# Linear attention and a Swish MLP on one core: batch 1's v loaded ahead of w_out's third quarter, its x transposed by DMA, batches 2 and 3 loaded behind it, batch 0's two norms back to back

## The chip, the cores and the metric

One Trainium2 chip, one of its cores. The engines go by short names: PE multiplies matrices, DVE (vectors) and ACT (exp, silu and the like) work on its results and inputs, POOL issues the loads and SP the stores and the DMA transposes. PSUM is the buffer that PE's products go to, which the kernel hands out in pairs of banks; SBUF is the memory that the loads fill. The granted clock is the share of its full rate that PE's clock was given. The metric is device time in microseconds (us) of one execution, median of several; lower is better. All experiments are timed beside the kernel before on the same chip; sets of runs were on different chips, so ratios are compared rather than times.

## The reference

```python
# q, k, v: (8, 8, 576, 64) f32; w_in: (512, 2048), w_out: (2048, 512), beta: (2048,)
def phi(x): return np.where(x > 0, x, np.exp(x) - 1.0) + 1.0
kv  = einsum('bhsd,bhse->bhde', phi(k), v)
num = einsum('bhsd,bhde->bhse', phi(q), kv)
den = einsum('bhsd,bhd->bhs', phi(q), sum(phi(k), axis=2)) + 1e-6
x = (num / den).transpose(0, 2, 1, 3).reshape(4608, 512)
h = x @ w_in
out = (h * sigmoid(beta * h)) @ w_out
```

## The kernel before

Names used below: **h(b)** is the first product of batch b (x times w_in, 16 slices of 128 columns of w_in, then silu on ACT), **y(b)** the second (g times w_out); **kv(b)** the 40 small products of phi(k) and v; **numerators** the products of phi(q) and kv, followed on DVE by the division (num_norm), which gives the normed rows; these must be transposed to become **x(b)**, the input of h(b). While the MLP of batch b runs on PE, the attention of batch b + 1 is slipped in between by a plan: at which step which function is emitted. The plan is read as the schedule: every engine is taken to do its work in the order of emission.

```python
def load_rows(dst, src, b, eng=nc.gpsimd):        # POOL's queue; f32 in memory, bf16 in SBUF
    eng.dma_start(out=dst[:, :, 0:NJ, :]..., in_=src[b, :, 0:MAIN, :]...)      # 512 KB
    eng.dma_start(out=dst[0:TAIL, :, NJ, :], in_=src[b, :, MAIN:S, :]...)      # 64 KB

def by_dma(b):
    return b >= DMA_T                              # DMA_T = 2: x(0), x(1) go through PE
def num_norm(b, t):
    ...                                            # den, reciprocal, xs = num * 1/den
    if by_dma(b) or t == NJ:
        nc.sync.dma_start_transpose(out=x_dst(b, t), in_=xs...)                # SP's queue
def x_trans(b, t, wide=False, dve=False):          # 4 PE transposes and one copy from PSUM
    ...
def h_last(b, x, between):                         # last 4 slices of h; they use the PSUM
    hps = []                                       # pairs that kv and numerators use too
    for i in range(2):
        hp = att_banks()
        for ii in range(2):
            h_mm(b, x, hp[:, ii], 12 + 2 * i + ii, 0, 4)
            hps.append(hp[:, ii])
    for f in between:
        f()                                        # exp of the next batch on ACT
    for i in range(4):
        silu(b, 12 + i, hps[i])                    # frees the PSUM pairs
def hold(a):
    nc.gpsimd.tensor_copy(held, a)                 # POOL, and so its loads, wait until a is there
# ... cut: start, h(0)
load_w_out(2)
load_v(1)
load_w_out(3)
# ... cut
load_next(2)                                       # k, q, v of batch 2
h_last(0, xT[0], [])
# ... cut: exp, relu, phi of batch 1
y_phase_wide(0, {
    4: [F(load_next, 3)],
    10: [F(q_trans, 1, 0, 1, 2, 3), F(kv_mm, 1), F(kv_evac, 1), F(w_out_scale, 3, 2)],
    11: [F(num_mm, 1, 0), F(num_norm, 1, 0)],
    12: [F(num_mm, 1, 1), F(num_norm, 1, 1), F(x_trans, 1, 0, wide=True)],
    # ... cut
})
h_phase(1, ...)
h_last(1, xT[1], [F(exp_, 2, 0), F(exp_, 2, 1)])   # exp of q(2), of k(2)
exp_(3, 1); exp_(3, 0); silu_table()
y_phase_wide(1, {
    1: [F(phi, 2, 0), F(q_trans_dma, 2), F(phi, 2, 1)],
    6: [F(kv_mm, 2), F(kv_evac, 2)],
    8: [F(num_mm, 2, 0), F(num_norm, 2, 0)],
    # ... cut
})
```

Of the kernel before, what the change touches and what calls it, by code (L numbers as in the profile page):

```python
# [16 lines left out]
def kernel(  # L17
# [12 lines left out]
    B, H, S, D = q.shape  # L30
# [3 lines left out]
    KC = DM // P  # L34
    FC = DFF // P
    NJ = 4
# [1 line left out]
    TAIL = S - MAIN  # L38
    NT = NJ + 1
    EA = D + 2  # L40
    DMA_T = 2
    TINY = 2.0 ** -30

    ctx.enter_context(tc.manual_schedule())
# [15 lines left out]
    HH = H // 2  # L60
# [5 lines left out]
    xT = [consts.tile([P, NJ, KC, P], BF16, name=f"xT{i}") for i in range(3)]  # L66
# [4 lines left out]
    def load_rows(dst, src, b, eng=nc.gpsimd):  # L71
        eng.dma_start(  # L72
            out=dst[:, :, 0:NJ, :].rearrange("p h j d -> p h (j d)"),
            in_=src[b, :, 0:MAIN, :].rearrange("h (p j) d -> p h (j d)", j=NJ),
        )
        eng.dma_start(
            out=dst[0:TAIL, :, NJ, :],
            in_=src[b, :, MAIN:S, :].rearrange("h s d -> s h d"),
        )

    def load_q(b):
        load_rows(xqk[b % NX][:, 0], q, b)

    def load_k(b):
        load_rows(xqk[b % NX][:, 1], k, b)

    def load_v(b):
        load_rows(vraw[b % 2], v, b)
# [19 lines left out]
    def load_w_out(i):  # L108
        for ii in range(2):
            c0 = 4 * i + 2 * ii  # L110
            nc.gpsimd.dma_start(out=w_out_f[i][ii], in_=w_out_v[:, c0 : c0 + 2, :])
# [92 lines left out]
        nc.vector.tensor_add(beta_c, beta_s, beta_m)  # L204
        nc.vector.reciprocal(rbeta, beta_c)

    def w_out_scale(i, on_dve=4):
        for c in range(4):
            ff = 4 * i + c
            dst, src, by = w_out_sb[i][:, c, :], w_out_f[i][c // 2][:, c % 2, :], rbeta[:, ff : ff + 1]  # L210
            if c < on_dve:
                nc.vector.tensor_scalar(dst, src, by, None, ALU.mult)
            else:
                nc.scalar.activation(dst, src, ACTF.Copy, scale=by)  # L214
# [1 line left out]

    st = {}

    def by_dma(b):
        return b >= DMA_T  # L220

    def begin(b):
        st[b, "p"] = work.tile([P, 2, NT, DM], BF16, tag="qk_p", name="qk_p")
# [17 lines left out]
    def phi(b, a, h0=0, h1=H):  # L241
        nc.vector.tensor_tensor(  # L242
            st[b, "p"][:, a].rearrange("p j (h d) -> p h j d", h=H)[:, h0:h1],
            st[b, "r", a][:, h0:h1], st[b, "e", a][:, h0:h1], ALU.min,
        )
# [9 lines left out]
    def work9(tag, **kw):  # L255
        return nine(work.tile([P, H, NT, D], BF16, tag=tag, name=tag, **kw), "jhd")

    def in9(a, j0, j1):
        if a == 1 and j0 >= KF:
            return k_last[:, :, j0 - KF : j1 - KF]  # L260
        return x9[a][:, :, j0:j1]

    def exp9(a, j0, j1):
        if j0 == 0:
            st["e9", a] = work9("e", bufs=3)
        nc.scalar.activation(
            st["e9", a][:, j0:j1].rearrange("p j h d -> p h j d"), in9(a, j0, j1),
            ACTF.Exp,
        )

    def relu9(a, j0, j1):
        if j0 == 0:
            st["r9", a] = work9("r")
        nc.vector.tensor_scalar(
            st["r9", a][:, j0:j1].rearrange("p j h d -> p h j d"), in9(a, j0, j1),
            0.0, 1.0, ALU.max, ALU.add,
        )
# [68 lines left out]
    def v_copy(b, h0=0, h1=H, dve=True):  # L346
        copy(
            vaug[b % 2][:, :, h0:h1, 0:D].rearrange("p j h d -> p h j d"),
            vraw[b % 2][:, h0:h1], dve,
        )  # L350
# [32 lines left out]
    def copy(dst, src, dve):  # L383
        if dve:
            nc.vector.tensor_copy(dst, src)  # L385
        else:
            nc.scalar.activation(dst, src, ACTF.Copy)  # L387
# [40 lines left out]
    def num_norm(b, t):  # L428
        n = P
        den = work.tile([P, 2, 4], F32, tag="den", name="den")  # L430
        rden = work.tile([P, 2, 4], F32, tag="rden", name="rden")
        xs = work.tile([P, 2, 4, D], BF16, tag="xs", name="xs", bufs=4)
        st[b, "xs", t] = xs
        nv = st[b, "n", t][:n, :, 0 : 4 * (D + 1)].rearrange("p a (h e) -> p a h e", h=4)
        nc.vector.tensor_scalar(den[:n], nv[:, :, :, D], 1e-6, None, ALU.add)  # L435
        nc.vector.reciprocal(rden[:n], den[:n])  # L436
        nc.vector.tensor_mul(  # L437
            xs[:n], nv[:, :, :, 0:D], rden[:n, :, :, None].to_broadcast([n, 2, 4, D])
        )
        if by_dma(b) or t == NJ:  # L440
            nc.sync.dma_start_transpose(
                out=x_dst(b, t), in_=xs.rearrange("p a h d -> p (a h d)")[:n]
            )
# [6 lines left out]
    def x_trans(b, t, wide=False, dve=False):  # L450
        n = P
        xv = st[b, "xs", t].rearrange("p a h d -> p (a h d)")
        tp = tr_bank(wide)[:, 0 : KC * P].rearrange("p (c n) -> p c n", c=KC)
        for p in range(KC):
            nc.tensor.matmul(  # L455
                tp[:, p, :n], xv[:n, p * P : (p + 1) * P], identity[:n, :n],
                is_transpose=True, start=True, stop=True, skip_group_check=True,
            )
        copy(x_dst(b, t), tp[:, :, :n], dve)
# [122 lines left out]
            y_out(b, t, yp[t], on_act=True)  # L582
            run(plan, 12 + t)

    def load_next(b):
        if b < B:
            load_k(b)
            load_q(b)
            load_v(b)

    held = consts.tile([1, 1], BF16)

    def hold(a):

        nc.gpsimd.tensor_copy(held, a)  # L595
# [14 lines left out]
    def warm(n):  # L610
        for _ in range(n):
            nc.tensor.matmul(  # L612
                st["warm"], g_sb[0][:, FC - 1, 0:P], g_sb[0][:, FC - 1, :],
                start=True, stop=True, skip_group_check=True,
            )

    def silu_table():
        nc.scalar.activation(small[:, 1:2], small[:, 0:1], ACTF.Silu)

    def F(f, *a, **k):  # L620
        return lambda: f(*a, **k)
# [31 lines left out]
    num_mm(0, 0)  # L653
    num_mm(0, 1)
    num_norm(0, 0)
    exp9(0, QF, N9)
    relu9(0, QF, N9)
    silu_table()
    warm(4)
    x_trans(0, 0, dve=True)  # L660
    num_norm(0, 1)
    phi9(0, QF, 6)
    phi9(0, 6, N9)
    qb2 = att_banks(BF16)


    load_w_out(2)
    load_v(1)
    load_w_out(3)

    def tidy():
# [3 lines left out]
    def q_rest():  # L675
        for t in range(2, NT):
            q_trans9(t, qb2, (t - 2) * 256)
        for t in range(2, NT):
# [5 lines left out]
        + [(ff, 0, 2) for ff in range(4, 8)] + [(ff, 2, 4) for ff in range(8)]  # L684
        + [(ff, 0, 4) for ff in range(8, 12)],
        {
            1: [F(x_trans, 0, 1)],
            3: [F(q_rest)],
            5: [F(num_mm, 0, 2), F(num_norm, 0, 2)],
            7: [F(num_mm, 0, 3), F(num_norm, 0, 3)],  # L690
# [5 lines left out]


    clear_tail(2)
    load_next(2)
    h_last(0, xT[0], [])  # L700
    begin(1)
    exp_(1, 1)
    exp_(1, 0)
    silu_table()
    relu(1, 1)
    relu(1, 0)
    w_out_scale(2)
    phi(1, 1)
    phi(1, 0)
    v_copy(1, 0, HH)  # L710
    v_copy(1, HH, H, dve=False)
    y_phase_wide(0, {
        4: [F(load_next, 3)],
        10: [
            F(q_trans, 1, 0, 1, 2, 3), F(kv_mm, 1), F(kv_evac, 1), F(w_out_scale, 3, 2),
        ],
        11: [F(num_mm, 1, 0), F(num_norm, 1, 0)],
        12: [F(num_mm, 1, 1), F(num_norm, 1, 1), F(x_trans, 1, 0, wide=True)],
        13: [F(num_mm, 1, 2), F(num_norm, 1, 2), F(x_trans, 1, 1, wide=True)],
        14: [F(num_mm, 1, 3), F(num_norm, 1, 3), F(q_trans, 1, 4)],  # L720
    })

    ALL = [(ff, 0, 4) for ff in range(FC)]
    h_phase(
        1, xT[1],
        [(ff, 0, 2) for ff in range(4)] + [(ff, 2, 4) for ff in range(4)] + ALL[4:12],
        {
            0: [F(x_trans, 1, 2), F(num_mm, 1, 4), F(num_norm, 1, 4)],
            1: [F(x_trans, 1, 3)],
            8: [F(begin, 2), F(relu, 2, 0)],  # L730
            10: [F(relu, 2, 1)],
            12: [F(v_copy, 2), F(load_v, 4)],
        },
    )
    begin(3)
# [3 lines left out]
    silu_table()  # L739
    y_phase_wide(1, {  # L740
        1: [F(phi, 2, 0), F(q_trans_dma, 2), F(phi, 2, 1)],
        6: [F(kv_mm, 2), F(kv_evac, 2)],
        8: [F(num_mm, 2, 0), F(num_norm, 2, 0)],
        9: [F(num_mm, 2, 1), F(num_norm, 2, 1)],
        10: [F(num_mm, 2, 2), F(num_norm, 2, 2)],
# [3 lines left out]
    for b in range(2, B + 1):  # L749
        n = b + 1  # L750
        groups = ALL
        plan = {}
        if b == 2:
            groups = (
                [(ff, 0, 2) for ff in range(8)] + [(ff, 2, 4) for ff in range(8)] + ALL[8:]
            )
        o = len(groups) - FC
        if n < B:
            plan[3 + o] = [F(relu, n, 0), F(phi, n, 0), F(q_trans_dma, n)]
            plan[5 + o] = [F(relu, n, 1), F(phi, n, 1)]  # L760
            plan[7 + o] = [F(v_copy, n), F(held_v, b + 3, n)]
            plan[12 + o] = [F(kv_mm, n)]
            plan[13 + o] = [F(kv_evac, n)]
        h_phase(b, xT[b % 3] if b < B else xT_tail, groups, plan)
        plan = {}
        if n + 1 < B:
            begin(n + 1)
            exp_(n + 1, 1)
            exp_(n + 1, 0)
        if n < B:  # L770
            for t in range(NT if n % 2 else NJ):
                plan[1 + 2 * t] = [F(num_mm, n, t)]
                plan[2 + 2 * t] = [F(num_norm, n, t)]
            plan[12] = [F(held_kq, b + 3, n)]
        y_phase(b, plan)
# [30 lines left out]
```

## Time and profile before

| | before |
|---|---|
| time, median of 3 runs (lowest to highest) | 292.67 us (292.13 to 292.94) |
| span of the profiled execution | 290.1 us |
| PE busy | 281.8 us (97%) |
| first h matmul / y(0) / h(1) / y(1) / h(2) starts on PE | 17.09 / 33.36 / 51.56 / 66.44 / 82.04 us |
| granted PE clock, mean | 0.994 |

The last row is from PE's timeline and serves as a ruler: what a stage costs is the distance between two of its entries.

### The profile page before, as it was taken

The numbers are of one execution on the slowest core, as the hardware profiler recorded it, in microseconds if no ns is written. First come the engines' busy times: TensorE is split into PE (matmuls) and PEld (weight loads), VectorE is DVE, ScalarE is ACT, GpSimd is POOL, SyncE is SP. The second block draws the span as 40 slices with busy tenths as digits, with TensorE's granted clock in tenths as the row PEclk, the third lists the DMA queues.
The fourth block names the chain that finished last, engine by engine and source line by source line (L and its number), as shares of the span: only waits on it lengthen the run. The fifth ranks groups of instructions, "written<-read, shape, count | busy, mean of one in ns | idle before, by whom it ended". The sixth has DMA issues, their size and how long they took to land.

```text
span 290.1 us, 4739 instructions
## 1 busy us (share of the span) xinstructions
PE 281.8 (97%) x1895; PEld 144.1 (50%) x1895; DVE 116.7 (40%) x235; ACT 174.0 (60%) x232; POOL 54.3 (19%) x79
## 2 busy tenths in 40 slices
PE   8889999999999999999999999999999999999994
PEld 3567445644576444454444444554455444444443
DVE  3784487504670365326532654163517300110021
ACT  2788798889998843875277617771750086018500
POOL 8924564400051205020402040000000000000000
PEclk9799999999999999999999999999999999999999
DMA  8999999999379956977894879433503500120033
GB/s 143 196 206 345 254 281 194 257 167 158 62 208 180 136 140 106 196 103 162 121 211 53 161 92 197 77 103 107 97 2 90 111 36 0 72 76 0 0 74 73
DMA packets 75766, 38.07 MB, mean 131 GB/s; under 512 B 43344, under 2 KB 70240, under 8 KB 75744
## 3 DMA queue, kind: packets, MB, share of 16 engines
q0 software_dynamic: 38912, 20.19, 49.0%
q1 hardware_dynamic: 36640, 17.44, 25.7%
q8 instruction: 15, 0.25, 0.4%
q10 hardware_dynamic: 192, 0.14, 0.2%
q14 instruction: 7, 0.06, 0.1%
HBM read 36.71 MB, written 9.44 MB: 159 GB/s over the span
## 4 chain that ended last, share of the span: by engine, by line
PE 92%; DMA 3%; POOL 3%; ACT 1%; issue 0%; DVE 0%; POOLq 0%
PE mm L527 42%; PE mm L475 41%; PE att L421 3%; DMA w_in<-in_moe_w_in_dram 3%; PE att L475 2%; PE att L362 2%; POOL xqk L135 1%; PE mm L559 1%; POOL vraw L135 1%; ACT q_pT L387 1%; PE mm L455 0%; PE att L395 0%; PE att L455 0%; DVE xT L385 0%; DVE y_sb L385 0%
## 5 line engine op out<-in xcount | busy, mean ns | idle before, releaser
L467 ACT ACTIVATE g<-mm,beta_c 128x512 bf16<-128x512 f32 (+2 forms) x160 | 97.8, 623 | 87.1 <-PE mm L475 87.0
L527 PE MATMUL mm<-w_out,g 128*128 128x512 bf16 x560 | 128.0, 379 | 0.0
L475 PE MATMUL mm<-xT,w_in 128*128 128x512 bf16 (+2 forms) x576 | 107.6, 344 | 1.3 <-DMA w_in<-in_moe_w_in_dram 1.2
L475 PEld LDWEIGHTS <-w_in 128*128 128x128 bf16 x672 | 63.8, 98 | 60.8 <-DMA w_in<-in_moe_w_in_dram 1.3
L527 PEld LDWEIGHTS <-g 128*128 128x128 bf16 x560 | 53.1, 98 | 59.0 <-issue 0.3
L537 DVE COPY y_sb<-mm 128x512 f32<-128x512 f32 x27 | 18.7, 692 | 72.9 <-PE mm L527 69.4
L229 ACT ACTIVATE e<-xqk 128x2560 bf16<-128x2560 bf16 x14 | 31.9, 2328 | 0.1
L242 DVE TENSOR_TENSOR qk_p<-r,e 128x2560 bf16<-128x2560 bf16 x14 | 20.8, 1491 | 12.8 <-ACT e L229 12.1
L437 DVE TENSOR_TENSOR xs<-att,rden 128x512 bf16<-128x512 f32 x36 | 24.9, 691 | 1.2
L372 DVE CAST kv_bd<-att 64x260 bf16<-64x260 f32 x14 | 6.0, 427 | 36.6 <-PE att L362 36.5
L435 DVE TENSOR_SCALAR den<-att 128x8 f32<-128x8 f32 x36 | 5.9, 163 | 26.8 <-PE att L421 26.8
L421 PEld LDWEIGHTS <-q_pT 128*128 128x128 bf16 (+1 forms) x160 | 11.1, 102 | 9.5 <-issue 1.3
L421 PE MATMUL att<-kv_bd,q_pT 128*128 128x130 bf16 (+1 forms) x160 | 14.8, 226 | 0.4 <-ACT q_pT L387 0.3
L475 PE MATMUL mm<-xT_tail,w_in 128*128 128x512 bf16 x64 | 14.0, 379 | 0.0
L595 POOL COPY held<-xT 1x1 bf16<-1x1 bf16 x4 | 2.0, 509 | 63.6 <-DMA xT<-xs 63.6
L237 DVE TENSOR_SCALAR r<-xqk 128x2560 bf16<-128x2560 bf16 x14 | 11.9, 853 | 4.0 <-DMA xqk<-in_q_dram 2.5
L612 PE MATMUL mm<-g 128*128 128x512 bf16 x30 | 9.3, 464 | 1.2 <-DVE g L145 1.2
L229 ACT ACT_TABLE_LOAD x7 | 9.0, 1283 | 0.1
L72 POOL DMA_DIRECT2D vraw<-in_v_dram x7 | 6.4, 909 | 10.1 <-DVE vaug L385 4.2
L72 POOL DMA_DIRECT2D xqk<-in_q_dram x7 | 7.1, 1021 | 3.9 <-ACT w_out L214 2.1
L436 DVE RECIPROCAL rden<-den 128x8 f32<-128x8 f32 x36 | 7.3, 203 | 1.2
L72 POOL DMA_DIRECT2D xqk<-in_k_dram x7 | 6.5, 935 | 5.3 <-DMA w_in<-in_moe_w_in_dram 2.5
(77 smaller groups left out, 138.1 us busy)
## 6 DMA issues: line engine op xcount, KB each, us to landing
out_dram<-y_sb SPq DMA_DIRECT2D x28, 256.0 KB, 2.4
xqk<-in_k_dram POOLq DMA_DIRECT2D x7, 512.0 KB, 9.0
xqk<-in_q_dram POOLq DMA_DIRECT2D x7, 512.0 KB, 10.7
vraw<-in_v_dram POOLq DMA_DIRECT2D x7, 512.0 KB, 12.2
w_in<-in_moe_w_in_dram POOLq DMA_DIRECT2D x4, 512.0 KB, 10.1
g<-in_moe_w_out_dram POOLq DMA_DIRECT2D x4, 512.0 KB, 10.9
out_dram<-y_sb SPq DMA_DIRECT2D x14, 128.0 KB, 5.2
xqk<-in_moe_w_out_dram POOLq DMA_DIRECT2D x2, 512.0 KB, 13.7
```

The costliest lines, as they stand in the source:

```text
L72: eng.dma_start(out=dst[:, :, 0:NJ, :].rearrange("p h j d -> p h (j d)"), in_=src[b, :, 0:MAIN, :].rearrange("h (p j) d -> p h (j d)", j=NJ),)
L229: nc.scalar.activation(st[b, "e", a][:, h0:h1], xqk[b % NX][:, a, h0:h1], ACTF.Exp)
L237: nc.vector.tensor_scalar(st[b, "r", a][:, h0:h1], xqk[b % NX][:, a, h0:h1], 0.0, 1.0, ALU.max, ALU.add)
L242: nc.vector.tensor_tensor(st[b, "p"][:, a].rearrange("p j (h d) -> p h j d", h=H)[:, h0:h1], st[b, "r", a][:, h0:h1], st[b, "e", a][:, h0: ...
L421: nc.tensor.matmul(nps[r0 : r0 + n, p // 2, c0 : c0 + 2 * (D + 1)], st[bb, "qT"][:, t, p, :n], kv_bd[bb % 2][:, p], start=True, stop=True, ...
L436: nc.vector.reciprocal(rden[:n], den[:n])
L437: nc.vector.tensor_mul(xs[:n], nv[:, :, :, 0:D], rden[:n, :, :, None].to_broadcast([n, 2, 4, D]))
L467: nc.scalar.activation(g_sb[b % 2][:, ff, c0:c1], hp[:, c0:c1], ACTF.Silu, scale=beta_c[:, ff : ff + 1],)
L475: nc.tensor.matmul(hp[:, c0:c1], w_in_sb[ff // 4][:, kc, (ff % 4) * P : (ff % 4 + 1) * P], x[:, t0:t1, kc, :] if b < B else x[:, kc, c0:c1 ...
L527: nc.tensor.matmul(yp, g_sb[b % 2][:, ff, t * P : (t + 1) * P], w_out_sb[ff // 4][:, ff % 4, :], start=(ff == 0), stop=(ff == FC - 1),)
L537: nc.vector.tensor_copy(y_sb, yp)
L612: nc.tensor.matmul(st["warm"], g_sb[0][:, FC - 1, 0:P], g_sb[0][:, FC - 1, :], start=True, stop=True, skip_group_check=True,)
```

## The change

Its intent: PE is the bound (97% busy), so x(1) leaves PE and goes through SP's DMA transposes like every later batch. So that these are not slowed by loads, all loads of batches 2 and 3 wait behind x(1) (load_late). So that x(1) is early enough, kv(1) moves from after the 11th group of y(0) to after the 8th, for which v(1) is loaded earlier. Apart from that, batch 0's second norm moves ahead so that its x is ready by the time w_in lands.

```diff
--- before.py
+++ after.py
@@ -38,7 +38,6 @@
     TAIL = S - MAIN
     NT = NJ + 1
     EA = D + 2
-    DMA_T = 2
     TINY = 2.0 ** -30
 
     ctx.enter_context(tc.manual_schedule())
@@ -204,11 +203,11 @@
         nc.vector.tensor_add(beta_c, beta_s, beta_m)
         nc.vector.reciprocal(rbeta, beta_c)
 
-    def w_out_scale(i, on_dve=4):
-        for c in range(4):
+    def w_out_scale(i, cs=range(4), dve=True):
+        for c in cs:
             ff = 4 * i + c
             dst, src, by = w_out_sb[i][:, c, :], w_out_f[i][c // 2][:, c % 2, :], rbeta[:, ff : ff + 1]
-            if c < on_dve:
+            if dve:
                 nc.vector.tensor_scalar(dst, src, by, None, ALU.mult)
             else:
                 nc.scalar.activation(dst, src, ACTF.Copy, scale=by)
@@ -216,8 +215,9 @@
 
     st = {}
 
-    def by_dma(b):
-        return b >= DMA_T
+    def by_dma(b, t):
+
+        return b > 0 or t == NJ
 
     def begin(b):
         st[b, "p"] = work.tile([P, 2, NT, DM], BF16, tag="qk_p", name="qk_p")
@@ -437,7 +437,7 @@
         nc.vector.tensor_mul(
             xs[:n], nv[:, :, :, 0:D], rden[:n, :, :, None].to_broadcast([n, 2, 4, D])
         )
-        if by_dma(b) or t == NJ:
+        if by_dma(b, t):
             nc.sync.dma_start_transpose(
                 out=x_dst(b, t), in_=xs.rearrange("p a h d -> p (a h d)")[:n]
             )
@@ -581,12 +581,6 @@
                 y_mm(b, yp[t], t, ff)
             y_out(b, t, yp[t], on_act=True)
             run(plan, 12 + t)
-
-    def load_next(b):
-        if b < B:
-            load_k(b)
-            load_q(b)
-            load_v(b)
 
     held = consts.tile([1, 1], BF16)
 
@@ -653,19 +647,20 @@
     num_mm(0, 0)
     num_mm(0, 1)
     num_norm(0, 0)
+    num_norm(0, 1)
     exp9(0, QF, N9)
     relu9(0, QF, N9)
+    warm(4)
+    x_trans(0, 0)
     silu_table()
-    warm(4)
-    x_trans(0, 0, dve=True)
-    num_norm(0, 1)
+    x_trans(0, 1, dve=True)
     phi9(0, QF, 6)
     phi9(0, 6, N9)
     qb2 = att_banks(BF16)
 
 
+    load_v(1)
     load_w_out(2)
-    load_v(1)
     load_w_out(3)
 
     def tidy():
@@ -684,7 +679,6 @@
         + [(ff, 0, 2) for ff in range(4, 8)] + [(ff, 2, 4) for ff in range(8)]
         + [(ff, 0, 4) for ff in range(8, 12)],
         {
-            1: [F(x_trans, 0, 1)],
             3: [F(q_rest)],
             5: [F(num_mm, 0, 2), F(num_norm, 0, 2)],
             7: [F(num_mm, 0, 3), F(num_norm, 0, 3)],
@@ -696,40 +690,44 @@
 
 
     clear_tail(2)
-    load_next(2)
     h_last(0, xT[0], [])
     begin(1)
     exp_(1, 1)
     exp_(1, 0)
-    silu_table()
     relu(1, 1)
     relu(1, 0)
-    w_out_scale(2)
     phi(1, 1)
+    v_copy(1)
     phi(1, 0)
-    v_copy(1, 0, HH)
-    v_copy(1, HH, H, dve=False)
     y_phase_wide(0, {
-        4: [F(load_next, 3)],
-        10: [
-            F(q_trans, 1, 0, 1, 2, 3), F(kv_mm, 1), F(kv_evac, 1), F(w_out_scale, 3, 2),
+        7: [
+            F(kv_mm, 1), F(w_out_scale, 2, (0, 1), False), F(q_trans, 1, 0, 1, 2, 3),
+            F(kv_evac, 1), F(w_out_scale, 2, (2, 3)),
         ],
-        11: [F(num_mm, 1, 0), F(num_norm, 1, 0)],
-        12: [F(num_mm, 1, 1), F(num_norm, 1, 1), F(x_trans, 1, 0, wide=True)],
-        13: [F(num_mm, 1, 2), F(num_norm, 1, 2), F(x_trans, 1, 1, wide=True)],
-        14: [F(num_mm, 1, 3), F(num_norm, 1, 3), F(q_trans, 1, 4)],
+        9: [F(num_mm, 1, 0), F(num_norm, 1, 0), F(w_out_scale, 3, range(4), False)],
+        10: [F(num_mm, 1, 1), F(num_norm, 1, 1)],
+        11: [F(num_mm, 1, 2), F(num_norm, 1, 2), F(silu_table)],
+        12: [F(num_mm, 1, 3), F(num_norm, 1, 3)],
+        13: [F(q_trans, 1, 4)],
     })
+
+    def load_late():
+        hold(xT[1][0:1, NJ - 1, KC - 1, 0:1])
+        for b in (2, 3):
+            load_k(b)
+            load_q(b)
+            if b == 2:
+                load_v(b)
 
     ALL = [(ff, 0, 4) for ff in range(FC)]
     h_phase(
         1, xT[1],
-        [(ff, 0, 2) for ff in range(4)] + [(ff, 2, 4) for ff in range(4)] + ALL[4:12],
+        [(ff, 0, 2) for ff in range(8)] + [(ff, 2, 4) for ff in range(8)] + ALL[8:12],
         {
-            0: [F(x_trans, 1, 2), F(num_mm, 1, 4), F(num_norm, 1, 4)],
-            1: [F(x_trans, 1, 3)],
-            8: [F(begin, 2), F(relu, 2, 0)],
-            10: [F(relu, 2, 1)],
-            12: [F(v_copy, 2), F(load_v, 4)],
+            0: [F(load_late), F(num_mm, 1, 4), F(num_norm, 1, 4)],
+            12: [F(begin, 2), F(relu, 2, 0)],
+            14: [F(relu, 2, 1)],
+            16: [F(v_copy, 2)],
         },
     )
     begin(3)
@@ -739,7 +737,7 @@
     silu_table()
     y_phase_wide(1, {
         1: [F(phi, 2, 0), F(q_trans_dma, 2), F(phi, 2, 1)],
-        6: [F(kv_mm, 2), F(kv_evac, 2)],
+        6: [F(kv_mm, 2), F(kv_evac, 2), F(held_v, 3, 2)],
         8: [F(num_mm, 2, 0), F(num_norm, 2, 0)],
         9: [F(num_mm, 2, 1), F(num_norm, 2, 1)],
         10: [F(num_mm, 2, 2), F(num_norm, 2, 2)],
@@ -758,7 +756,7 @@
         if n < B:
             plan[3 + o] = [F(relu, n, 0), F(phi, n, 0), F(q_trans_dma, n)]
             plan[5 + o] = [F(relu, n, 1), F(phi, n, 1)]
-            plan[7 + o] = [F(v_copy, n), F(held_v, b + 3, n)]
+            plan[7 + o] = [F(v_copy, n), F(held_v, n + 1, n)]
             plan[12 + o] = [F(kv_mm, n)]
             plan[13 + o] = [F(kv_evac, n)]
         h_phase(b, xT[b % 3] if b < B else xT_tail, groups, plan)
```

## The prediction

> **What bounds the kernel now.** I read the busy table first, then the chain that ended last in order of time, then the timelines of ACT and of SP's queue, and last the landing times of single transfers.
>
> ```profile
> span 290.1 us, 4739 instructions
> PE 281.8 (97%) x1895; PEld 144.1 (50%) x1895; DVE 116.7 (40%) x235; ACT 174.0 (60%) x232; POOL 54.3 (19%) x79
> ```
>
> PE is busy 97% of the span. That alone could hide pipelined overlap, so I trust the chain more:
>
> ```profile
> 9.03 8.02 DMA w_in<-in_moe_w_in_dram
> 17.05 0.05 issue
> 17.09 0.62 PE mm L475 x8
> 17.71 0.22 PE mm L455 x4
> ...
> 33.53 9.50 PE mm L527 x44
> 43.02 0.91 PE att L395 x16
> 43.93 0.02 issue
> 43.95 1.95 ACT q_pT L387 x2
> 45.90 0.04 issue
> 45.94 0.39 PE att L421 x4
> ...
> 47.77 0.34 PE att L455 x4
> ```
>
> Until 17.05 us the first w_in load sets the time; from there on the chain is PE work almost without a break (PE has 92% of it). The reader sees the only large exception, 1.95 us of ACT copies. Kv products and four y products run beside them, so PE itself stands still for only some 0.4 us there and 0.3 us a little later, waiting for w_out's last quarter. So all that can be gained is PE work removed or these small gaps; anything the change delays past PE's need is lost one for one.
>
> What can be delayed is data. Each line gives one transfer of a q matrix's transpose through SP's queue, its start, and the time to landing (first alone but for the end of one load, then beside loads of k and q):
>
> ```profile
> L407 SPq DMA_TRANSPOSE q_pT<-qk_p x1: 3077/3077/3077, 69.1 to 69.1; - x1
> DMA to landing us min/median/max: 4.8/4.8/4.8
> ```
>
> ```profile
> L407 SPq DMA_TRANSPOSE q_pT<-qk_p x1: 5927/5927/5927, 144.8 to 144.8; - x1
> DMA to landing us min/median/max: 9.8/9.8/9.8
> ```
>
> [...] k, q, v of batch 3 and v of batch 4 (issued 43.8, 47.6, 50.7, 56.4 us; 17.4, 16.6, 16.5, 13.9 us to landing) land at 61.2, 64.2, 67.2, 70.3, so one each 3.05 us. Each is 576 KiB as bf16 and twice that as read: 1.18 MB / 3.05 us = 387 GB/s. [...] the 128x512 transposes of x land in 2.4 us when nothing else moves[...].
>
> **The change part by part.**
>
> *Batch 0's norms back to back.* One transpose group of x (four, 0.22 us on the chain at 17.71) goes into the wait for w_in. The second norm (DVE 0.17 + 0.20 + 0.69, about 1.05 us) then ends near 16.1, the transposes at 16.5, still before 17.05. The silu table load now follows a copy of x and ends near 18.0 in place of 16.6, but with four banks of PSUM, PE only needs the first silu at about 18.3. ACT loses one x copy (0.5 us) and a 0.5 us wait for q's copies. Gain: about 0.5 us, so the first y phase starts at 33.0 in place of 33.5.
>
> *v(1) before w_out's third quarter.* q(1) lands at 36.5; v(1) then follows one load later, 39.6, in place of 42.1. The two w_out quarters take 1.2 us per half, so the last still lands near 44.5.
>
> *kv(1) after the 8th group in place of the 11th.* PE is there at 33.0 + 32 x 0.216 = 39.9. ACT's exp of k and q starts after the silus and a table load, 35.6, and takes 2 x 2.3: 40.3. DVE: phi(k) ends 39.5, v's copy (0.82) 40.5, phi(q) (1.49) 42.0. So PE waits about 0.6 us for v, runs kv (0.75) and waits 0.75 us again for phi(q): 1.4 us lost, where the old order lost 0.75. The two old waits should go: the first numerator now takes the PSUM pair that kv left, not the one q's copies still hold. w_out's last quarter, now 4 x 0.72 us on ACT after q's copies, is just ready (47.8) when PE wants it. Net -0.65 us.
>
> *x(1) by DMA.* Sixteen PE transposes go, 4 x 0.23 us = 0.9 us of chain. The 256-column groups that replace four 512-column ones cost PE nothing (0.109 against 0.216 us each). SP's order puts the fourth transpose behind the first two stores, which wait for ACT's first y copy (49.9): it starts at 51.1 and lands near 53.5; the half of h that needs it starts at 54.8. No wait.
>
> Sum up to the second y phase: 0.5 - 0.65 + 0.9, plus about 0.6 us of pieces that disappear (x copies on ACT, PE's changes to and from transposes): about 1.4 us gained, its start moves from 66.6 to 65.2. For this alone I would say 291.3.
>
> *Loads of batches 2 and 3 behind x(1).* Here is the cost. The hold is released at 53.5, k(2) is issued near 54.1. A k load with quiet queues took 6.5 us (issued 111.4), so k(2) lands at 60.6 or later with the stores of batch 0 beside it, then one load each 3.1 us: q(2) 63.8, v(2) 67.0, k(3) 70, q(3) 73. Before, all of batch 2 was there at 54.7. exp(q) can still start at 64.3. But on DVE v(2)'s copy stands ahead of phi(q): 67.9, phi 69.4, and q's transpose starts near 69.5 (before 69.1) with 3.6 us of loads still to run, like the one at 144.8, which had some 3.9 us of loads left. So it takes 8 to 9.8 us where it took 4.8: landing 77.5 to 79. PE reaches the first numerator of batch 2 at 65.2 + 9 x 0.863 + 0.75 = 73.7; before it ran at 75.2 with the data there since 73.9. PE would stand 4 to 5 us, and the net against before would be 77.8 - 75.2 = +2.6 us at face value. After this stage nothing returns: loads of v one step later still land some 20 us ahead of use.
>
> **The rivals.**
>
> 1. *The late loads are in time.* If the fourth x lands at 52, or q's transpose [...] lands in 5 us (74.5), the wait is under 1 us and the gain of up to 1.4 us stays: 291.3 to 292. For it: the transpose is small beside the loads, and 4.8 us was seen with one load still moving. Against: four later ones took 9.8 to 10.3 us beside loads.
> 2. *The loads take still longer.* The stores of batch 0 (1.2 MB) stood between v(2) and k(3) before, which landed 6.5 us apart and not 3.1. If they collide with k(2), everything moves 1 to 3 us: 296 to 298. Against: most stores leave before k(2) has data moving.
> 3. *The new wait at kv(1) is the bigger one*, if v(1) does not keep 39.6 but 41: another 1.4 us, though the loads' wait later would hide part of it, being counted from x(1)'s arrival only in part.
> 4. *Nothing moves*: gain and wait cancel, 292.7.
>
> **Range and chances.** The face value is 292.7 + 2.6 = 295.3. The landing has an error of some 2 us either way and the result a floor at -1.4 us when the wait vanishes; I give rival 1 about 35%, since whoever put the loads there will have looked at this very transpose. Weighted: 0.35 x 291.6 + 0.65 x 295.3 = 294.0. The range of 8 in 10 is 290.4 to 297.6. A 2% gain (286.8) would need more than all gaps and removed work that I find; a 2% loss (298.5) needs rival 2 in full: 3% and 7%, and 90% for within 2%.
>
> **What would show it.** Right: the chain around 41 shows DVE phi or v's copy between PE pieces; no transposes of x(1) on PE; the second y phase starts near 65; around 74 to 78 the chain leaves PE for the DMA of q's transpose, whose landing is 8 us or more. Wrong: PE unbroken from 65 to 85 with that landing near 5 us (rival 1), k(2) landing after 63 (rival 2), a PE wait at the h phase on x(1)'s transpose or on the silu table at 18, which I rule out, or a wait in a later batch.

Its sum: 0.5 - 0.65 + 0.9 + 0.6, about 1.4 us gained up to y(1); the late data turn this into +2.6, so 295.3 at face value and 294.0 after the lean towards rival 1. The 0.6 (pieces that disappear) is an estimate; of PE's changes to transposes the trace shows 0.34 and 0.23 us from the start of numerators to that of the transposes behind them (at 47.37 and 48.81 us), against 0.24 us to y products (at 45.94). The one load each 3.1 us is the spacing of four landings, and the 8 to 9.8 us of q's transpose an estimate from the one at 144.8; why transposes take longer beside loads was not shown.

## More of the kernel before

The lines that carry the reading are in the prediction. One more belongs here, the granted clock in 40 slices of the span (9 is 90% or more):

```profile
PEclk9799999999999999999999999999999999999999
```

## The result, and the profile after

The changed kernel took 297.13 us, median of 4 (296.67 to 297.48), the kernel before 292.81 (4 runs): ratio 1.0149, interval 1.0125 to 1.0173. Ratios are the mean time of one kernel's fast runs over that of the other's of the same rounds, so not quite the ratio of the medians quoted. In a later set of runs (e12) it was 1.0195. So it is slower by 1.5 to 2%: clear of the noise, though at a threshold of 2% the verdict on record is "same" here and "unclear" for e12.

| PE's timeline, us | before | after | difference of the stage |
|---|---|---|---|
| first h matmul | 17.09 | 16.55 | -0.54 (w_in landed sooner in this execution) |
| y(0) starts | 33.36 | 32.59 | -0.23 |
| h(1) starts | 51.56 | 50.58 | -0.21 |
| y(1) starts | 66.44 | 64.94 | -0.52 |
| kv(2) starts | 72.57 | 74.99 | **+3.92** |
| first numerator of batch 2 | 75.06 | 78.86 | **+1.38** |
| h(2) starts | 82.04 | 86.81 | **+0.97** |
| end of span | 290.1 | 294.6 | -0.3 |

Up to y(1) the changed kernel is 1.5 us ahead, and it loses 6.3 us in the next 22 us. Neither part before nor part after takes part in the loss. PE's timeline of the kernel before at this place (start, duration, engine, line, operation, tiles, shapes, count):

```profile
66.44 6.21 PE L527 MATMUL mm<-w_out,g 128*128 128x512 bf16 x28
72.57 0.82 PE L362 MATMUL att<-vaug,qk_p 128*64 128x65 bf16 x40
73.33 1.90 PE L527 MATMUL mm<-w_out,g 128*128 128x512 bf16 x8
```

and of the changed one, with the idle time ahead of a piece and what ended it in brackets:

```profile
64.94 6.21 PE L527 MATMUL mm<-w_out,g 128*128 128x512 bf16 x27
74.99 0.82 PE L362 MATMUL att<-vaug,qk_p 128*64 128x65 bf16 x40 [3.85 <-ACT g L467]
75.97 3.10 PE L527 MATMUL mm<-w_out,g 128*128 128x512 bf16 x7 [0.16 <-issue]
```

Two things are to be seen. PE stands 3.85 us ahead of kv(2), and the wait is put down to a silu of batch 1 on ACT. And behind the wait eight y products (one record is missing) take 3.10 us, where the same eight took 1.90. The second is the clock. The windows of the changed kernel give, after the window and its length, the busy times of PE, PEld (PE's weight loads), DVE, ACT and POOL, then the granted clock, the DMA share (the time of packets over that of the 16 DMA engines; it can pass 1) and GB/s:

```profile
74.00:76.00 2.00, 0.85 (x41) 0.89 (x43) 0.15 (x1) 2.00 (x4) 0.00 (x0) 1.00 1.52 201
76.00:78.00 2.00, 2.00 (x5) 0.68 (x5) 0.70 (x2) 1.97 (x3) 0.00 (x0) 0.51 0.83 186
78.00:80.00 2.00, 2.00 (x10) 1.09 (x9) 0.39 (x3) 2.00 (x2) 1.55 (x3) 0.63 0.03 8
```

The clock is halved for some 3 us after the wait (granted 1.00, 0.53, 0.50, 0.50, 0.77 and 1.00 in the stretches of 1 us from 75 to 81 us), which is nearly the whole of the +1.38. That it falls behind a wait of PE is what this trace shows (0.51 from 76 to 78 us, behind 3.85 us); from which length on it does so is not shown, and waits of like length went both ways in the experiments (list at the end).

Why was a silu so late? The chain that ended last, of the changed kernel, in order of time (start, duration, what):

```profile
53.51 0.18 POOL held L589
...
55.55 0.87 POOL xqk L71
56.42 10.01 DMA xqk<-in_q_dram
...
70.04 2.32 ACT e L229
...
72.38 1.28 ACT L467
...
74.26 0.69 ACT g L467
74.95 0.04 issue
74.99 0.82 PE att L362 x40
75.81 0.16 issue
75.97 3.10 PE mm L527 x7
...
81.98 4.69 DMA xT<-xs
```

It reads from top to bottom as one string of waits. The hold lets go at 53.5; q(2) is issued and lands at 66.4; ACT, which has exp of q(2) as next in its order, then loads its table (1.28 us) and runs the two exps until 72.4; another table load (1.28 us); and only then the silus of batch 1's last slices, which free the PSUM pair that kv(2) needs, at 74.95. PE wants it at 71.15. In the kernel before q(2) was there at 50.6, and ACT's exps ran from 65.2 to 69.7. The last line is a smaller wait of 0.5 us at h(2), for x(2)'s transposes, which here run beside the load of v(3).

The other part of the change did what it was meant to. The fourth transpose of x(1), start and time to landing, in the changed kernel:

```profile
L441 SPq DMA_TRANSPOSE xT<-xs x1: 1240/1240/1240, 51.0 to 51.0; - x1
DMA to landing us min/median/max: 2.4/2.4/2.4
```

### The profile page after: what moved, and what is told of

Its sections match the earlier page's. It is cut to its first block, busy times and chain, and to the rows that moved or that the text cites. A ratio compares the mean times of both kernels' runs of the same rounds, so it can differ in the third digit from the quotient of the medians.

```text
span 294.6 us, 4739 instructions
## 1 busy us (share of the span) xinstructions
PE 279.8 (95%) x1874; PEld 144.2 (49%) x1895; DVE 114.9 (39%) x231; ACT 174.5 (59%) x235; POOL 53.5 (18%) x82
## 4 chain that ended last, share of the span: by engine, by line
PE 70%; DMA 13%; issue 9%; POOL 4%; ACT 2%; DVE 1%; POOLq 0%; ACTq 0%
PE mm L475 33%; PE mm L527 33%; DMA xqk<-in_k_dram 5%; DMA xqk<-in_q_dram 3%; DMA w_in<-in_moe_w_in_dram 3%; PE att L421 2%; DMA xT<-xs 2%; PE att L362 2%; POOL xqk L134 1%; PE mm L559 1%; POOL vraw L134 1%; ACT e L229 1%; POOL g L110 1%; POOL xqk L71 1%; DVE xs L437 0%
## 5 line engine op out<-in xcount | busy, mean ns | idle before, releaser
L475 PEld LDWEIGHTS <-w_in 128*128 128x128 bf16 x688 | 65.3, 98 | 59.4 <-DMA xT<-xs 1.0
L527 PEld LDWEIGHTS <-g 128*128 128x128 bf16 x560 | 53.5, 98 | 59.2 <-issue 1.3
L589 POOL COPY held<-q_pT 1x1 bf16<-1x1 bf16 x5 | 0.9, 176 | 54.8 <-DMA q_pT<-qk_p 54.8
L362 PE MATMUL att<-vaug,qk_p 128*64 128x65 bf16 x280 | 5.8, 196 | 4.2 <-ACT g L467 3.8
L606 PE MATMUL mm<-g 128*128 128x512 bf16 x29 | 8.5, 443 | 1.3 <-DVE g L144 1.2
L362 PEld LDWEIGHTS <-qk_p 128*64 128x64 bf16 x280 | 5.1, 111 | 7.2 <-DVE qk_p L242 3.3
```

Source lines behind the costliest of these rows:

```text
L362: nc.tensor.matmul(kvp[g * D : (g + 1) * D, p, :], st[b, "p"][:, 1, j, c0 : c0 + D], vaug[b % 2][:, j, 2 * p + g, 0 : D + 1], start=(j == ...
L475: nc.tensor.matmul(hp[:, c0:c1], w_in_sb[ff // 4][:, kc, (ff % 4) * P : (ff % 4 + 1) * P], x[:, t0:t1, kc, :] if b < B else x[:, kc, c0:c1 ...
L527: nc.tensor.matmul(yp, g_sb[b % 2][:, ff, t * P : (t + 1) * P], w_out_sb[ff // 4][:, ff % 4, :], start=(ff == 0), stop=(ff == FC - 1),)
L606: nc.tensor.matmul(st["warm"], g_sb[0][:, FC - 1, 0:P], g_sb[0][:, FC - 1, :], start=True, stop=True, skip_group_check=True,)
```

## The experiments

Three theories were set up first. **L**: the late loads of batch 2 are the loss. **X**: the loads had to go because x(1) by DMA cannot live beside them, so the root is x by DMA. **O**: the new order of kv(1), q(1) and w_out costs by itself.

| run | what | median us | ratio to before (interval) |
|---|---|---|---|
| e1_loads_early | changed, all loads early | 297.03 | 1.0171 (1.0148 to 1.0194) |
| e2_late_only | before, loads late | 297.25 | 1.0187 (1.0153 to 1.0221) |
| e3_batch2_early | changed, batch 2's loads early | 298.42 (one run slow) | 1.0262 (1.0197 to 1.0327), see e3 |
| e4_silu_first | changed, silus ahead of exps | 298.35 | 1.0224 (1.0169 to 1.0280) |
| e5_x_on_pe | changed, loads early, x(1) on PE | 292.34 | 1.0013 (0.9996 to 1.0029) |
| e6_hold_third | changed, hold 1 part earlier | 297.31 | 1.0178 (1.0153 to 1.0204) |
| e7_norms_only | before, norms back to back | 291.80 | 1.0006 (0.9979 to 1.0033) |
| e8_hold_second | changed, hold 2 parts earlier | 298.75 | 1.0248 (1.0209 to 1.0286) |
| e9_q_first | changed, q(2) loaded ahead of k(2) | 299.07 | 1.0233 (1.0206 to 1.0260) |
| e10_reordered | e9, silus first, v's copy last | 297.08 | 1.0165 (1.0137 to 1.0192) |
| e11_q_first_v_last | e9, v's copy last | 299.41 | 1.0252 (1.0234 to 1.0270) |
| e12_changed_again | the changed kernel | 297.45 | 1.0195 (1.0173 to 1.0216) |

### e1: the changed kernel with the loads early

```diff
+    load_next(2)                      # ahead of h_last(0, ...)
     y_phase_wide(0, {
+        4: [F(load_next, 3)],
-            0: [F(load_late), F(num_mm, 1, 4), F(num_norm, 1, 4)],
-            16: [F(v_copy, 2)],
+            0: [F(num_mm, 1, 4), F(num_norm, 1, 4)],
+            16: [F(v_copy, 2), F(load_v, 4)],
-        6: [F(kv_mm, 2), F(kv_evac, 2), F(held_v, 3, 2)],
+        6: [F(kv_mm, 2), F(kv_evac, 2)],
-            plan[7 + o] = [F(v_copy, n), F(held_v, n + 1, n)]
+            plan[7 + o] = [F(v_copy, n), F(held_v, b + 3, n)]
```

> The changed kernel with every load of batches 2, 3 and 4 put back where the kernel before has it (no hold on x(1)). Theory L (the late loads are the whole loss): q(2) lands near 50 us again, PE's wait at the kv products of batch 2 (3.85 us) and the low clock behind it (1.7 us) go, and what is left is the 1.5 us that the changed kernel was ahead at the second y phase: about 291.3 us, 0.995 of before. Rival X (x(1) by DMA cannot live beside the loads, which is why they were held): the four transposes of x(1) take 4 to 8 us in place of 2.4, the first or second half of h(1) waits for them by 2 to 5 us, and the time is 293 to 296. Rival O (the loss lies in the new order of kv(1), q(1), w_out): about 296 to 297 as changed.

297.03 us, no better than the changed kernel. The wait at kv(2) is gone, as L said, and another has come. The fourth transpose of x(1), to be set against the 2.4 us above:

```profile
L441 SPq DMA_TRANSPOSE xT<-xs x1: 1249/1249/1249, 51.9 to 51.9; - x1
DMA to landing us min/median/max: 8.5/8.5/8.5
```

and what it does to PE at the start of h(1), from e1's PE timeline:

```profile
49.60 1.69 PE L527 MATMUL mm<-w_out,g 128*128 128x512 bf16 x7
55.51 1.01 PE L475 MATMUL mm<-xT,w_in 128*128 128x256 bf16 x4 [4.23 <-DMA xT<-xs]
```

Each of the four transposes took 7.5 to 8.5 us beside the loads; PE waited 4.23 us for the second, and again the clock fell behind it (0.67 granted from 54 to 58 us; four 128x256 products in 1.01 us where 0.60 is usual). So X holds for this kernel, though the time lies above X's 293 to 296 and where O expected it; the trace tells the two apart, and e5 again. L alone is refuted as a repair: taking the late loads away gives nothing back.

### e2: the kernel before with the loads late

```diff
-    load_next(2)
-        4: [F(load_next, 3)],
+    def load_late(): ...              # as in the change
-            1: [F(x_trans, 1, 3)],
-            12: [F(v_copy, 2), F(load_v, 4)],
+            1: [F(x_trans, 1, 3), F(load_late)],
+            12: [F(v_copy, 2)],
-        6: [F(kv_mm, 2), F(kv_evac, 2)],
+        6: [F(kv_mm, 2), F(kv_evac, 2), F(held_v, 3, 2)],
-            plan[7 + o] = [F(v_copy, n), F(held_v, b + 3, n)]
+            plan[7 + o] = [F(v_copy, n), F(held_v, n + 1, n)]
```

> The kernel before with only the loads of batches 2 and 3 held until x(1) is complete (here written by ACT, near 54.3 us), v(3) behind batch 2's q transpose. Theory L: q(2) lands near 67, ACT's exp of batch 2 waits for it, the silus behind it end 3 us late, PE waits about 3 us at kv(2) and runs slow after it: 296.5 to 298.5 us, 1.013 to 1.02 of before. Rival O or X: the held loads alone cost under 1 us, since without x(1) by DMA the queues are less full: 293 to 293.7.

297.25 us, inside what L expected. Its PE timeline has the wait of the changed kernel, then one of 0.55 us at the first numerator for q's transpose, then this at h(2):

```profile
74.52 0.82 PE L362 MATMUL att<-vaug,qk_p 128*64 128x65 bf16 x40 [2.42 <-ACT g L467]
...
86.95 13.13 PE L475 MATMUL mm<-xT,w_in 128*128 128x256 bf16 x84 [2.08 <-DMA xT<-xs]
```

The clock fell behind the last one: 0.88 granted from 84 to 88 us, 0.69 from 88 to 92. (The profile is of its longest run, 298.54 us.) So the late loads suffice for the loss, without x(1) by DMA. With e1 it makes half of a square: either part alone costs some 5 us, and so do both together.

### e3: batch 2's loads early, batch 3's held

```diff
+    load_k(2); load_q(2); load_v(2)   # ahead of h_last(0, ...)
     def load_late():
         hold(xT[1][0:1, NJ - 1, KC - 1, 0:1])
-        for b in (2, 3): ...
+        load_k(3); load_q(3)
```

> The changed kernel with batch 2's k, q, v issued early as before, and only batch 3's k and q held until x(1) has landed. Theory L: batch 2 lands by 55 us, no PE wait at kv(2); its q transpose near 69 is beside no loads; 291.0 to 291.5. Rival X: batch 2's loads (44 to 55 us) beside the transposes of x(1) make h(1) wait 1 to 4 us: 292 to 295. Against e1 this tells whether batch 3's loads matter for the transposes.

298.42 us with the slow run in it; the three fast runs took 295.89, 298.03 and 298.81, a median above either range, and the fourth (301.93) was slow. The ratio, 1.0262, is what the three longest runs give, the slow one among them; the three fast ones over the mean of before's runs (291.95) give 1.019, which is the number to use. Its profile is of its shortest run and shows X: PE waited 3.80 us at h(1) for x(1). What made the spread, its one profile does not show; mean granted clocks of 0.988 against 0.992 go with it. Batch 2's three loads alone are enough to make x(1) late.

### e4: silus ahead of the exps

```diff
-    h_last(1, xT[1], [F(exp_, 2, 0), F(exp_, 2, 1)])
+    h_last(1, xT[1], [])
+    exp_(2, 0)
+    exp_(2, 1)
```

> The changed kernel, loads still late, but the last four silus of batch 1 stand ahead of batch 2's exps on ACT, so PSUM is free near 65 us and not 74.9. Theory A (PE's wait at kv(2) is for PSUM that ACT frees late, in the same queue behind exp that waits for q(2)): the wait shrinks to that for phi(k), DVE at about 73.2 to 74: 1 to 2 us come back, but then the numerators wait for q's transpose (landed 78.1), so the end is 295 to 296.5. Rival (the data alone bounds, PSUM is no matter): 297 as changed. If all 4.4 us came back (292.7 or less), lateness of the loads would not be the cause but the order on ACT.

298.35 us (fast runs from 296.55 to 300.70), above the 295 to 296.5 expected and nearer to the rival's 297: nothing came back. With PSUM free early, PE waited 2.87 us at the same kv(2), now for phi(k) on DVE, 1.85 us at h(2) for x(2), and the clock fell to 0.50 between. So the order on ACT decides what PE is seen to wait for, and not whether it waits.

### e5: e1 with x(1) on PE again

```diff
-        return b > 0 or t == NJ
+        return b > 1 or t == NJ
-        10: [F(num_mm, 1, 1), F(num_norm, 1, 1)],
-        11: [F(num_mm, 1, 2), F(num_norm, 1, 2), F(silu_table)],
+        10: [F(num_mm, 1, 1), F(num_norm, 1, 1), F(x_trans, 1, 0, wide=True, dve=True)],
+        11: [F(num_mm, 1, 2), F(num_norm, 1, 2), F(x_trans, 1, 1, wide=True, dve=True), F(silu_table)],
-            0: [F(num_mm, 1, 4), F(num_norm, 1, 4)],
+            0: [F(x_trans, 1, 2), F(num_mm, 1, 4), F(num_norm, 1, 4)],
+            1: [F(x_trans, 1, 3)],
     # and the loads as in e1
```

> e1 (the changed kernel with all loads early) and x(1) transposed on PE again, its first two copies on DVE. In e1 PE waited 4.2 us at h(1) for transposes of x(1) that took 7.5 to 8.5 us beside the loads, 2.4 to 2.5 us without. Theory D (x(1) by DMA is the root: it either waits for the engines or pushes the loads back): no wait at h(1) and none at kv(2), 0.9 us of PE transposes come back: 291.0 to 292.2, 0.996 to 1.000 of before. Rival (what is left of the change, v(1) first, kv(1) earlier, norms, itself costs): 293 or more, with PE waits at 40 to 43 us above the 1.0 us seen.

292.34 us, 1.0013, the same as before within its interval (just above the expected 291.0 to 292.2, below the rival's 293). No wait is left at h(1), kv(2) or h(2), and the clock is 9 in all slices. This closes the square: with x(1) on PE and early loads 1.001, x(1) by DMA alone 1.017, late loads alone 1.019 (e2, built on the old order of the rest), both 1.015 to 1.020. Theory O falls with it: v(1) first, kv(1) earlier and the norms together cost nothing that can be told, and gain nothing.

### e6 and e8: the hold let go earlier

```diff
-        hold(xT[1][0:1, NJ - 1, KC - 1, 0:1])
+        hold(xT[1][0:1, NJ - 2, KC - 1, 0:1])     # e6; in e8 the index is 1
```

> The changed kernel, but the hold ahead of the late loads waits for the third part of x(1) (landed 50.9 us in its trace) and not the fourth (53.4): loads 2.6 us earlier. Theory L: q(2) lands near 63.9, the chain q(2), exp, silu, free PSUM ends near 72.3 against PE's arrival at 71.1: wait about 1.2 in place of 3.85 us[...]; 292.2 to 293.3. Rival X: the fourth transpose (issued 51.0) now lies beside the loads, takes 7 us, h(1) waits about 4 us: 295 or more.

> As e6, but the hold waits for the second part of x(1) (landed 49.6): loads 3.9 us earlier than in the changed kernel. Theory L: q(2) lands near 62.6, no wait at kv(2); if the fourth transpose still lands in time 291.0 to 291.8. Rival X as in e6, here stronger: the third and fourth lie beside loads, h(1) waits 2 to 4 us: 293.5 to 296.

Neither came back: 297.31 and 298.75 us. In e6 the loads went out at 52.2 in place of 54.0, but the fourth x took 4.6 us, PE waited for x(1) 0.98 us, for PSUM at kv(2) 2.15 us and for x(2) 2.21 us; and q(2) landed no earlier (ACT's exp could start at 66.8). In e8 (loads at 50.7) the fourth x took 7.9 us, as X expected. PE waited no more at kv(2), but not for L's reason: q(2) landed at 67.7 and not at 62.6, later than in the changed kernel, and PE itself came to kv(2) only at 78.6, behind a wait of 4.25 us at h(1) and a low clock (0.50 granted from 58 to 62 us, 0.67 from 62 to 66):

```profile
L441 SPq DMA_TRANSPOSE xT<-xs x1: 1218/1218/1218, 51.7 to 51.7; - x1
DMA to landing us min/median/max: 7.9/7.9/7.9
```

```profile
59.60 9.58 PE L475 MATMUL mm<-xT,w_in 128*128 128x256 bf16 x48 [4.25 <-DMA xT<-xs]
```

So letting the loads go 1.8 and 3.3 us earlier brought q(2) in no earlier (66.4 us in the changed kernel, 66.8 in e6, 67.7 in e8); it only set loads beside the transposes of x(1). The wait moves from kv(2) to h(1), and none of it goes. The gains that L expected of both did not come; e6 is where its rival put it (295 or more, though with a shorter wait at h(1)), e8 lies above even its rival's 293.5 to 296.

### e7: the norms alone

```diff
     num_norm(0, 0)
+    num_norm(0, 1)
     ...
-    silu_table()
     warm(4)
-    x_trans(0, 0, dve=True)
-    num_norm(0, 1)
+    x_trans(0, 0)
+    silu_table()
+    x_trans(0, 1, dve=True)
-            1: [F(x_trans, 0, 1)],
```

> The kernel before with the two norms of batch 0 back to back and nothing else. By the trace of the changed kernel PE comes to the first y phase 16.0 us after its first w_in matmul against 16.3 in the kernel before: 0.2 to 0.3 us faster, 0.999 of before. The prediction's figure was 0.5 us (0.998).

1.0006, interval 0.9979 to 1.0033: a gain of 0.2 us can neither be shown nor excluded. Four of six runs were at 291.35 to 291.93, two at 293.2 and 293.7.

### e9, e10, e11: can the engines' order live with late loads?

```diff
# e9: q(2) ahead of k(2)
-            load_k(b)
-            load_q(b)
+            for load in (load_q, load_k) if b == 2 else (load_k, load_q):
+                load(b)
# e11: e9, and v's copy behind both phis on DVE
-            16: [F(v_copy, 2)],
-        1: [F(phi, 2, 0), F(q_trans_dma, 2), F(phi, 2, 1)],
+        1: [F(phi, 2, 0), F(q_trans_dma, 2), F(phi, 2, 1), F(v_copy, 2)],
# e10: e11, and the silus first as in e4
```

> The changed kernel, loads as late as in it, but of batch 2 q is loaded ahead of k. This leaves x(1)'s transposes alone. Theory L says the waits lie in series: q(2) at about 62 in place of 66.4 lets ACT's exp of q start near 63; k(2) at 66.4 the exp of k at once behind it (69), silus free PSUM at 72.2 and not 74.9; but v(2)'s copy (landed 69.4) still stands ahead of both phis on DVE, phi(k) ends at 73.9 and q's transpose starts at 71.8 and lands at 78 as before. So kv(2) starts at 74 and the numerators wait for q's transpose: only 0.5 to 2 us come back: 295 to 296.5. Rival (the load of q is the one late thing): all 5.6 us of wait and slow clock go, 291.5.

> As e9, and ACT's last four silus of batch 1 ahead of batch 2's exps, and v(2)'s copy behind both phis on DVE. Theory L: every member of the series is freed: silus done at 65, exp(q) 63 to 66, q's transpose starts near 68 and lands at 74 to 77, phi(k) near 71, v's copy near 71; kv(2) at 71.1 to 71.9 without a real wait, numerators wait 0 to 3 us for q's transpose: 291.5 to 294.5. If it is still 296 or more, the late loads hurt in a way that the series does not hold (for example the later waits at h(2) for x(2)).

> The changed kernel with q of batch 2 loaded ahead of k and v's copy behind both phis on DVE, but batch 2's exps ahead of the last silus on ACT, as in the changed kernel. In e10 the silus first were a mistake: they wait for PE until 65.4, so the exps began at 68.2. Here exps start near 65.8 as in e9, q's transpose at 69.6 in place of 72.8, phi(k) ends near 72, v's copy near 72.8. Theory L (a series of waits behind the late loads): kv(2) waits 1 to 1.8 us, the numerators 0 to 2.5 us for q's transpose: 293.5 to 296, between before and changed. Were the order on the engines the cause and not the loads, it would come to 292 or less.

All three missed on the slow side of what was expected: 299.07, 297.08, 299.41 us. In e9 PE waited 2.94 us for phi(k) at kv(2) and then 3.71 us at the first numerator for q's transpose. In e10 the silus first were my mistake: they need the last products of h(1), which PE ends at 65.4, so the exps began at 68.2 and kv(2) waited 3.5 us, until v's copy, now behind phi(k) (74.27), was done at 75.01; h(2) then waited 2.25 us for x(2). In e11 kv(2) at last did not wait at all (it ran at 71.06). Then came this; first q's transpose, then PE:

```profile
L407 SPq DMA_TRANSPOSE q_pT<-qk_p x1: 6917/6917/6917, 68.4 to 68.4; - x1
...
DMA to landing us min/median/max: 11.6/11.6/11.6
```

```profile
80.02 0.61 PE L421 MATMUL att<-kv_bd,q_pT 128*128 128x130 bf16 x4 [6.31 <-DMA q_pT<-qk_p]
```

Started 3.4 us earlier than in the changed kernel (71.8 us), q's transpose landed 2 us later (80.0 in place of 78.0), most likely since more of k(3) and q(3) still stood in the queues beside it (q(3) landed at 77.3). PE waited 6.31 us and ran at half clock (0.50) from 80 to 84 us. Curing one wait exposed a longer one. This is the strongest sign that the transfers are the cause and not the order on ACT or DVE.

### e12: the changed kernel again

> The changed kernel itself, on the same chip as e11 and beside the same runs of the kernel before, since the runs that it was scored by were on another: 1.015 of before, 296.3 to 297.3 us; with it e11, and through the runs of before e9 and e10, can be set side by side.

297.45 us, 1.0195: the ratio is outside the expected 1.015 and its time just above. The profile has the same 3.8 us ahead of kv(2), and 1.2 us at h(2). The runs of before were shorter in that set (291.94), and mean clocks of the changed kernel went from 0.983 to 0.994 over its runs.

## Why the prediction was right or wrong

The time (294.0, range 290.4 to 297.6) was on the right side, and 297.13 lies near the upper end of the range. But the loss forecast was 1.3 us (2.6 before the lean towards rival 1) and the one measured 4.3. That late data of batch 2 would make PE stand between y(1) and h(2) was right; which wait, and how long, was not, so the time inside a wide range is partly luck. Point by point:

- **Up to y(1): right.** Predicted 65.2, measured 64.94. Of the gain of 1.5 us, 0.54 is w_in landing sooner in this one execution, so the change itself gave 0.96 and not 1.4, and the close hit is in part luck. The step of the norms was mis-sized: 0.5 predicted, 0.23 in the trace, not to be told in e7. The waits around kv(1) came as named: 0.36 us for v's copy and 0.67 for phi(q), 1.03 in place of 1.4. (The profile puts the second down to a w_out piece on ACT, done at 41.48; phi(q) was done at 41.45, and e1 and e5, with the same order here, put it down to phi.)
- **x(1) by DMA in time: right** (51.0 to 53.4; predicted 51.1 to 53.5). That the loads had to be away for it was not predicted as a need; e1 shows it.
- **The hold and the lateness of the loads: right in kind, too small.** k(2) issued 53.99 (predicted 54.1), but q(2) landed at 66.4 and not 63.8, v(2) near 69 and not 67. The term that was short is the one load each 3.1 us: k(2) landed at 61.2, 0.6 us late, but q(2) 5.2 us behind it. Batch 0's last store (landed 63.4) and the transpose of x(1)'s tail (65.8) were moving beside it, which is like rival 2, but its own sign, k(2) after 63, did not come, and no run moved the stores: the reason is not shown.
- **Where PE would wait: wrong by one step.** The prediction had "PE reaches the first numerator of batch 2" and waits there 4 to 5 us for q's transpose. Measured: PE waits 3.85 us earlier, at kv(2), for PSUM that silus free behind the exps of the late q(2). The prediction followed DVE and SP's queue and left out that ACT takes exp, table and silu in one order, which had only some 0.3 us to spare in the kernel before (first pair of silus done near 72.3, kv(2) at 72.57). q's transpose landed at 78.0, inside the predicted 77.5 to 79, but by two errors that cancel: it started at 71.8 in place of 69.5 and took 6.2 us in place of 8 to 9.8. That was 0.9 us ahead of need (78.86), hidden by the new wait; e11 laid it bare, with 6.31 us.
- **What was not foreseen: the clock.** It is most of the +1.38 us between kv(2) and the numerators, and a little after it. Added to the face value (295.3) it gives some 296.7, near the time measured, but this sum is made afterwards and takes the predicted wait for the one that came; the lean towards rival 1 (35%) pulled the point the wrong way.
- **Nothing returns after this stage: right.** From h(2) to the end the two kernels differ by 0.3 us.
- **Where the expected gain went:** removing 16 PE transposes can win 0.9 us at most (the prediction's estimate), and took 7.7 us without loads beside them (45.7 to 53.4). Those could not be had for nothing: holding the loads back for so long made batch 2 late.

Left open: how much of the spread of the slower kernels (up to 4.4 us among the fast runs of e3, e4 and e8) is the clock; whether the norms gain 0.2 us; why q(2), loaded behind k(2), lands at 66 to 68 us however early the hold is let go. No version tried beats the kernel before.

## What to carry to other kernels

Before a transfer is held back to keep another one quiet, follow what needs it through every engine's order to the next PE instruction, the PSUM release too: the least slack of these is what may be spent. A small DMA transpose was cheap here only in quiet queues (2.4 us, against 8.5 beside loads), so taking 0.9 us of transposes off a bound PE may cost more than it gives. And a PE wait may cost more than its length: of the ten waits between 2.8 and 6.4 us in these profiles, from h(1) to h(2), seven went with a fall of the clock (to 0.50 in four, 0.67 in e1 and 0.78 in e12 as means of 4 us, 0.8 in the slices of e9) and three did not (3.51 and 3.80 us left it at 1.00, and behind 2.94 us eight y products took the usual 1.90 us); one of only 2.08 us (e2) went with a fall too (0.69).

## What the traces show of the transfers and the clock

- A 128x512 transpose went from 2.4 to 2.5 us to 7.5 to 8.5 us beside loads (e1), and the 128x2560 one from 4.8 (before) to 11.6 us (e11).
- The 128x2560 bf16 transpose (655 KB) took 4.8 us with little beside it, 137 GB/s, issue and landing included. Against x's transposes (131 KB in 2.4 us) the further 524 KB took 2.4 us, an estimate of 218 GB/s for these alone.
- One wait of 3.80 us (e3) and one of 3.51 (e10) left the clock at 1.00, one of 3.78 (e12) did not (0.79 granted from 72 to 76 us, 0.78 from 76 to 80); one of 2.87 us (e4) was followed by 0.68, then 0.50, and one of 2.08 us (e2, at h(2), with full products on both sides) by 0.69 from 88 to 92 us, where 2.21 and 2.25 us at the same place (e6, e10) left it at 1.00. So the length of a wait alone does not tell whether the clock falls; what else does is not shown.
- Loads in a row read 387 GB/s here, an estimate worked out in the prediction from landings 3.05 us apart.
